# First head loaded and prepared in two parts, hash bits with a padded pitch, and two re-timed feed schedules in an attention + MoE kernel

## The chip, the cores and the metric

The kernel runs on one core of one Trainium2 chip. Engines are called as in the profile: PE is TensorE, PEld its weight loads, DVE is VectorE, ACT is ScalarE, POOL is GpSimd, SP issues most DMAs.

## The reference

Hash attention (4 batches, 8 heads, 768 tokens, head size 64) followed by a gated two-layer product on the attention output. Queries and keys are put in buckets by the signs of six projections; a query sees only the keys of its own bucket.

```python
q_bits = einsum('bhsd,dk->bhsk', q, proj) > 0          # same for k; 6 bits make a bucket
scores = where(q_bucket == k_bucket, q @ k.T / 8, -1e9)
attn   = exp(scores - max);  attn /= attn.sum() + 1e-9
x      = (attn @ v) -> [3072 tokens, 512]
h      = x @ w_in                                      # 512 -> 2048
out    = (h * sigmoid(h)) @ w_out                      # 2048 -> 512
```

## The kernel before

The work is a list of 288 units `w` (32 heads, nine units each). A unit is one score of 512 columns, one exponential on ACT, and four products with v ("AV") on PE. The sign bits of q and k are stacked under the values as extra rows, so one matmul gives value score and bucket test together. Everything else (transposes, bit projections, the MoE products of the batch before) is hung between the units: `plan(w, fn)` at fixed units, `moeq` as a queue of MoE pieces.

```python
def load_first(h):                       # first two heads: rows of q and k, on the SP queue
    for n, src in (("q", q), ("k", k)):
        nc.sync.dma_start(out=qk_sb[0, n][:, h], in_=src[0, h]...)
...
def proj_unit(*pairs):                   # bits of two pairs of heads, 768 columns
    bt = btp.tile([P, S], F16, tag="bits", name="bits")
    ...                                  # two PSUM tiles bp_ps (tag "m", 3 buffers), signs by DVE
def bits_unit(pairs, i, par):            # copy 13 x 768 bits under the values, on DVE
    nc.vector.tensor_copy(out=dst, in_=bits[pairs][r, :])
...
def mm1(ci, grp):                        # h = x @ w_in: 4 matmuls of 512 columns,
    hp = ps.tile([P, f, n], F32, tag="m", name="h_ps", bufs=3)   # same 3 PSUM buffers
    ...                                  # tanh on ACT, then g = (th + 1) * h on DVE
...
# the start: no unit can run before head 0's bits are there
t_first(0, 0, nc.scalar.copy); t_first(0, 1, nc.vector.tensor_copy)    # transposes of head 0
warm_up(2); bt = proj_first(0); v_unit(0, (0,))
...                                      # casts, bit copies of head 0
t_first(1, 0, nc.scalar.copy); t_first(1, 1, nc.vector.tensor_copy)    # transposes of head 1
warm_up(3)
...
for w in range(NW):                      # 3 scores lead
    for fn in at.pop(w, []): fn()
    ...
    skip = w % 3 == 2 or w % QST in (20, 21)    # QST = 36, BST = 72 units a batch
    if n == 1 and len(moeq) - keep < left and skip: n = 0
    for _ in range(n): moeq.popleft()()
    av(w); score(w + LEAD)
```

The softmax here doesn't subtract the row's maximum and nothing guards it: scores larger than these inputs give would overflow.

## Time and profile before

| | before |
|---|---|
| median | 306.18 us (305.82 to 306.61, 3 runs) |
| span of the profiled run | 304.06 us |
| bit copies on DVE (13 x 768) | 14 at 534 ns, 7 at 627 ns, 7 at 594 ns |

PE does something nearly all the time, so I measure everything by position: when the AV of a given unit starts. Four stretches follow: the start (up to the AV of unit 1, 10.29 us), units 1 to 54 (30.37 us), units 54 to 144 (71.77 us: the first quarter of MoE work has to be fitted in here), and the rest (191.63 us).

### The profile page before, as it was taken

To read this page: it belongs to the slowest core of one execution; us is meant where nothing else is said; L and a number is where in the kernel's file an instruction comes from. 1 tells how busy PE (TensorE), PEld (TensorE's weight loads), DVE (VectorE), ACT (ScalarE), POOL (GpSimd) and SP (SyncE) were. 2 spreads that over 40 slices of the span, in tenths; PEclk is the share of its full clock that TensorE was granted. 3 is DMA by queue.
4 is the path that set the end of the run, shared out by engine and by line. 5 is a ranking of instruction groups with operands and counts; after the bars stand their busy time and mean duration, and the time that the engine had idled before them with its cause. 6 is when DMAs were issued, how large, how long until landed. Compare 5 with 4: busy or idle time off the path is not lost.

```text
span 304.1 us, 7165 instructions
## 1 busy us (share of the span) xinstructions
PE 299.6 (99%) x2710; PEld 174.9 (58%) x2710; DVE 180.7 (59%) x341; ACT 210.7 (69%) x392; POOL 129.2 (42%) x203
## 2 busy tenths in 40 slices
PE   8999999999999999999999999999999999999996
PEld 3675855555666545555565665555566654446653
DVE  5697977799559344854696334853543442664332
ACT  5987989988877696978976766878877732442300
POOL 7589999377506851855148321765111100000000
PEclk9999999999999999999999999999999999999999
DMA  7999898999979838854068246011022013001112
GB/s 204 242 241 195 179 149 127 226 160 99 165 133 187 137 77 237 127 113 133 2 115 125 76 63 197 5 42 32 2 60 63 0 38 95 34 2 69 37 63 75
DMA packets 102786, 32.87 MB, mean 108 GB/s; under 512 B 90656, under 2 KB 99808, under 8 KB 102752
## 3 DMA queue, kind: packets, MB, share of 16 engines
q1 hardware_dynamic: 98368, 28.22, 44.6%
q0 software_dynamic: 4224, 4.19, 9.1%
q8 instruction: 21, 0.34, 0.5%
q14 instruction: 13, 0.11, 0.1%
q10 hardware_dynamic: 160, 0.00, 0.0%
HBM read 27.27 MB, written 6.29 MB: 110 GB/s over the span
## 4 chain that ended last, share of the span: by engine, by line
PE 95%; DVE 3%; ACT 1%; issue 0%; POOL 0%; ACTq 0%; POOLq 0%
PE h_ps L423 26%; PE o_ps L455 26%; PE s_ps L333 20%; PE o_ps L365 13%; PE bp_ps L279 3%; PE tp_ps L185 2%; PE o_ps L441 1%; PE warm_ps L125 1%; DVE g L429 1%; DVE qka L310 1%; ACT u L336 1%; PE bp_ps L225 1%; PE tp_ps L198 1%; PE o_ps L356 0%; DVE bits L285 0%
## 5 line engine op out<-in xcount | busy, mean ns | idle before, releaser
L336 ACT ACTIVATE u<-s_ps 128x512 f16<-128x512 f32 x288 | 156.4, 602 | 39.9 <-PE s_ps L333 39.4
L429 DVE SCALAR_TENSOR_TENSOR g<-th,h_ps 128x512 f16<-128x512 f32 x96 | 65.1, 683 | 75.4 <-ACT th L427 75.4
L423 PE MATMUL h_ps<-xT,win 128*128 128x512 f16 (+1 forms) x512 | 97.4, 325 | 0.1
L365 PEld LDWEIGHTS <-u 128*128 128x128 f16 x1152 | 67.6, 98 | 42.9 <-ACT u L336 11.2
L455 PE MATMUL o_ps<-wout,g 128*128 128x512 f16 x368 | 91.6, 379 | 0.0
L365 PE MATMUL o_ps<-vv,u 128*128 128x65 f16 x1152 | 82.8, 194 | 0.3
L427 ACT ACTIVATE th<-h_ps 128x512 f32<-128x512 f32 x96 | 57.3, 597 | 36.6 <-PE h_ps L423 33.5
L423 PEld LDWEIGHTS <-win 128*128 128x128 f16 x512 | 49.9, 98 | 31.8 <-issue 0.4
L385 POOL TENSOR_TENSOR x_pr<-osum,rec 128x384 f16<-128x384 f32 x23 | 19.0, 826 | 89.4 <-DVE rec L384 89.0
L455 PEld LDWEIGHTS <-g 128*128 128x128 f16 x368 | 35.8, 98 | 34.1
L333 PE MATMUL s_ps<-qka 71*128 71x512 f16 x192 | 52.7, 327 | 0.2 <-DVE qka L238 0.2
L333 PE MATMUL s_ps<-qkb 128*128 128x512 f16 x192 | 52.8, 326 | 0.0
L251 POOL TENSOR_SCALAR qka<-qk 64x1536 f16<-64x1536 f32 x15 | 22.0, 1465 | 12.1 <-DVE qk L246 6.8
L460 DVE TENSOR_SCALAR osb<-o_ps 128x512 f32<-128x512 f32 x23 | 15.8, 686 | 15.5 <-PE o_ps L455 15.5
L251 POOL TENSOR_SCALAR qkb<-qk 64x1536 f16<-64x1536 f32 x15 | 22.1, 1471 | 1.2
L262 POOL TENSOR_TENSOR vsa<-v_sb 128x192 f32<-128x192 f32 x32 | 19.3, 604 | 0.0
L260 POOL CAST vv<-v_sb 128x384 f16<-128x384 f32 x32 | 16.7, 520 | 0.9 <-DMA v_sb<-in_v_dram 0.5
L333 PEld LDWEIGHTS <-qka 71*128 71x128 f16 x192 | 15.4, 97 | 0.8 <-ACT qka L238 0.6
L246 DVE STREAM_TRANSPOSE qk<-k_blk 128x768 f32<-128x768 f32 x10 | 15.8, 1576 | 0.0
L246 DVE STREAM_TRANSPOSE qk<-q_blk 128x768 f32<-128x768 f32 x10 | 15.7, 1572 | 0.0
L333 PEld LDWEIGHTS <-qkb 128*128 128x128 f16 x192 | 15.4, 97 | 0.0
L379 DVE TENSOR_TENSOR osum<-o_ps,vsum 128x390 f32<-128x390 f32 x23 | 13.0, 565 | 2.3
(64 smaller groups left out, 164.8 us busy)
## 6 DMA issues: line engine op xcount, KB each, us to landing
out_dram<-osb SPq DMA_DIRECT2D x23, 256.0 KB
v_sb<-in_v_dram SPq DMA_DIRECT2D x15, 384.0 KB
q_blk<-in_q_dram SPq DMA_DIRECT2D x40, 96.0 KB
k_blk<-in_k_dram SPq DMA_DIRECT2D x40, 96.0 KB
win<-in_moe_w_in_dram POOLq DMA_DIRECT2D x4, 512.0 KB, 8.1
wout<-in_moe_w_out_dram POOLq DMA_DIRECT2D x4, 512.0 KB, 8.1
q_sb<-in_q_dram SPq DMA_DIRECT2D x5, 384.0 KB
k_sb<-in_k_dram SPq DMA_DIRECT2D x5, 384.0 KB
```

Source lines behind the costliest of these rows:

```text
L246: nc.vector.transpose(out=dst, in_=qk_sb[p, "qk"[n]])
L251: nc.gpsimd.tensor_scalar(out=dst[rows, :], in0=qk32[p][rows, :], scalar1=CS, scalar2=1.0, op0=ALU.mult, op1=ALU.mult)
L260: nc.gpsimd.tensor_copy(out=vv[:, :, 0:D], in_=src)
L262: nc.gpsimd.tensor_tensor(out=sa, in0=src[:, 0:3], in1=src[:, 3:6], op=ALU.add)
L333: nc.tensor.matmul(sp[:, o0 : o0 + n], t[rows, S + jt * P : S + (jt + 1) * P], t[rows, c0 : c0 + n], start=True, stop=True)
L336: nc.scalar.activation(out=u, in_=sp, func=AF.Exp, scale=ESC)
L365: nc.tensor.matmul(o_ps[h][:, c0 // P + i, :], u[:, o0 + i * P : o0 + (i + 1) * P], vv[:, jt, :], start=(not direct(h) and w % NU == 0 and ...
L385: (nc.vector if direct(h) else nc.gpsimd).tensor_tensor(out=x_pr[p][:, :, par * D : (par + 1) * D], in0=o[:, 0:NJ, 0:D], in1=rec[:, :, Non ...
L423: nc.tensor.matmul(hp[:, j, :], w_in16[:, dt, ft * P : (ft + 1) * P], xT[4 * b + dt][:, c0 : c0 + n], start=(dt == 0), stop=(dt == NDT - 1))
L427: nc.scalar.activation(out=th, in_=hp, func=AF.Tanh, scale=0.5)
L429: after.append(lambda: nc.vector.scalar_tensor_tensor(out=g[ci][:, grp * f : (grp + 1) * f, :], in0=th, scalar=1.0, in1=hp, op0=ALU.add, o ...
L455: nc.tensor.matmul(o2[tt], g[ci][:, ft, ct * P : (ct + 1) * P], w_out16[:, ft, :], start=(ft == 0), stop=(ft == NFT - 1))
```

## The change

Its intent: start the scores sooner by loading head 0 in two parts (two of three tile pairs first) with k on ACT's DMA queue beside q on SP's; keep DVE's bit copies to one port (the prediction says why), by giving the bits a pitch of 258; and fill two places where PE waits for ACT, by opening two MoE groups early (three of their four matmuls at units 66 and 70) and by spreading batch 1's MoE pieces evenly. The diff, cut:

```diff
 def load_first(h):
+    for c in ((slice(0, 4 * D), slice(4 * D, NJ * D)) if h == 0 else (slice(0, NJ * D),)):
         for n, src in (("q", q), ("k", k)):
-            nc.sync.dma_start(out=qk_sb[0, n][:, h], ...
+                (nc.scalar if (h, n) == (0, "k") else nc.sync).dma_start(
+                    out=qk_sb[0, n][:, h, c], ...
-    nc.scalar.dma_start(out=pw..., in_=proj)      # twice
+    nc.gpsimd.dma_start(out=pw..., in_=proj)      # twice, after the identity
...
-        bt = btp.tile([P, S], F16, tag="bits", name="bits")
+        bt = btp.tile([P, 3, CB + 2], F16, tag="bits", name="bits")      # CB = 256
-                nc.vector.tensor_copy(out=dst, in_=bits[pairs][r, :])
+                nc.vector.tensor_copy(out=dst, in_=bits[pairs][r, :, 0:CB])
...
-        def mm1(ci, grp):
+        def mm1(ci, grp, dts=slice(0, NDT)):      # may leave a group open after 3 of 4
...
-    t_first(0, 0, nc.scalar.copy)
-    t_first(0, 1, nc.vector.tensor_copy)
+    xa, xb = slice(0, 2), slice(2, 3)
+    t_first(0, 0, act, xa)                        # casts, k, then t_rest() for xb,
+    ...                                           # signs and bit copies by part
-    t_first(1, 0, nc.scalar.copy)                 # head 1 before the first scores
-    t_first(1, 1, nc.vector.tensor_copy)
+    plan(0, lambda: t_first(1, 0, act))           # head 1 behind them
+    plan(0, lambda: t_first(1, 1, vec))
-        plan(w0 + 20, lambda Q=Q: proj_unit(2 * Q, 2 * Q + 1))
+        wp = w0 + (24 if Q == 2 else 20)          # units 56 -> 60
+        plan(wp, lambda Q=Q: proj_unit(2 * Q, 2 * Q + 1))
+    for i in range(2):
+        plan(66 + 4 * i, first_units[0].pop(0))   # the two opened groups
...
         skip = w % 3 == 2 or w % QST in (20, 21)
+        if BST + 5 <= w < 2 * BST:
+            skip = w * 36 // 66 == (w - 1) * 36 // 66
```

I call its parts S (start), B (bits), H (opened groups), W (projection at unit 60) and P (even spacing); each can be applied alone.

## The prediction

> **What bounds the kernel now.** I read the page's busy table and chain of waits first, then a table of stretches, then the waits of two stretches, last the timeline of the first 10 us.
>
> ```profile
> PE 299.6 (99%) x2710; PEld 174.9 (58%) x2710; DVE 180.7 (59%) x341; ACT 210.7 (69%) x392; POOL 129.2 (42%) x203
> PE 95%; DVE 3%; ACT 1%; issue 0%; POOL 0%; ACTq 0%; POOLq 0%
> ```
>
> TensorE carries 95% of the chain. So the time is the first matmul (1.01 us), plus all TensorE work, plus every pause of TensorE, plus a tail of about 3 us. The change removes no TensorE work; it can only remove pauses and start earlier. Matmul busy (99%) hides the pauses because matmuls overlap, so I look where matmuls wait for weights, in the stretches where ScalarE (ACT) is full:
>
> ```profile
> 31.00:44.50 13.50, 13.50 (x180) 9.58 (x177) 11.69 (x19) 12.22 (x25) 12.66 (x16) 1.00 0.99 157
> 44.50:53.00 8.50, 8.48 (x105) 4.33 (x102) 6.33 (x15) 8.50 (x19) 7.87 (x18) 1.00 0.84 126
> ...
> 107.50:113.00 5.50, 5.39 (x62) 2.55 (x61) 2.13 (x7) 5.21 (x11) 3.54 (x8) 1.00 0.17 55
> ```
>
> The columns are us, then the busy time of PE, PEld, DVE, ACT, POOL. The first row is for contrast: ACT has 1.3 us to spare. From 44.5 to 53 ACT is busy 8.50 of 8.50 us and weight loads only 4.33; from 107.5 to 113 ACT has 5.21 of 5.50. The waits of these two stretches, in order:
>
> ```profile
> PEld L365 <- ACT u L336: 3.9, 15, 0.3
> ```
> ```profile
> PEld L365 <- ACT u L336: 2.6, 9, 0.4
> ```
>
> There the product with v (AV) waits for the exponential. One unit of attention is one exponential (ACT: 22 in 10.93 us, 0.50 each) but only a 512-column score and four AV matmuls on TensorE: in the timeline an AV group at 12.12 is followed by its score at 12.23 and the next work at 12.46, so 0.34. Between 44.05 and 53.15 lie 19 units: 9.10 - 19 x 0.34 - 0.67 (six transposes, two starting matmuls) = 2.0 us of pause. Between 107.87 and 112.43 lie 9: 4.56 - 9 x 0.34 = 1.5 us. A third such place, six units from 27.91 to 30.78, has 2.87 - 6 x 0.34 = 0.8 us. After 113 us I find none worth naming. Outside the start, then, some 5 us of pauses are all there is.
>
> The start:
>
> ```profile
> 1.01 2.31 PE L125 MATMUL warm_ps<-warm 128*128 128x512 bf16 x5 [1.01 <-POOL warm L114]
> ...
> 3.31 0.87 PE L198 MATMUL tp_ps<-ident,q_row 128*128 128x128 f32 x3
> ...
> 4.22 0.48 ACT L201 COPY qk<-tp_ps 128x384 f32<-128x384 f32 x1 [0.74 <-PE tp_ps L198]
> ...
> 6.44 0.68 DVE L228 TENSOR_SCALAR bits<-bp_ps,sc 128x384 f16<-128x384 f32 x1 [0.96 <-PE bp_ps L225]
> ...
> 7.15 0.70 DVE L238 COPY qka<-bits 7x384 f16<-7x384 f16 x2
> ...
> 8.00 0.81 PE L333 MATMUL s_ps<-qka 71*128 71x512 f16 x4 [0.16 <-DVE qka L238]
> ...
> 9.51 0.85 PE L225 MATMUL bp_ps<-qk,pw 128*32 128x384 f32 x8
> ...
> 10.29 0.30 PE L365 MATMUL o_ps<-vv,u 128*128 128x65 f16 x4
> ```
>
> A chain of dependent steps leads from the landing of q (transposes at 3.31) to the first score at 8.00. The second unit's AV starts at 10.29, behind head 1's bit projection (9.51).
>
> **What the Trainium skill says.** "TensorE: Matmul & The Clock Gate", section "What's actually happening": the array runs at half rate until about 3.4 us of activity. The trace agrees: five warm-ups of 512 columns start 0.43 us apart from 1.01, while 512-column matmuls later take 0.215 (four in 0.86 in the chain). "VectorE: DVE Perf Modes", section "What auto-detection actually checks": a 16-bit copy within SBUF takes four elements a cycle only if the outermost counts of source and destination are both even, or equal. "SBUF — State Buffer", section "Who interferes with whom": such a two-port copy excludes GpSimd for the whole instruction. The trace agrees: the 13x768 bit copies have minimum 351 ns, maximum 1591 ns, the long ones while GpSimd ran its 1465 ns casts. "DMA: Bandwidth & Descriptors", section "Issuing engines are not separate DMA queues": a second queue saves issue time only. Before, the SP issues of q and k start at 0.75 and 1.21, so 0.46 us is what it can save.
>
> **The change part by part.**
>
> Start, first head. Two of three tile pairs go first; k is issued by ACT beside q. The warm-ups (21 blocks of 128 columns at 0.107) keep TensorE until 1.01 + 2.25 = 3.25, so the q transposes start at about 3.25, no earlier than before. From there, sizes scaled from the rows above: second q transpose at 3.47, ACT copy 3.92 to 4.29 (256 columns, 0.37 instead of 0.48), k transposes to 4.12 and DVE copy 4.57 to 5.0; the last tile pair's transposes and a warm-up hold TensorE to 5.3; projection of 256 columns, bits ready at about 6.05 (before 6.44). Signs 0.53 instead of 0.68, two bit copies of 0.25 instead of 0.35: 7.2. First score at about 7.3, 0.7 earlier.
>
> But the second score needs q's last tile pair: signs of 128 columns (0.4) and two small copies (0.2 each) come behind on DVE, so 8.1 to 8.2. Exponentials then start at 7.7, 8.6 and 9.1. Head 1's transposes (6 x 0.109 = 0.65) were before done while TensorE waited for the bits; now they follow the third score, and the ACT copy of them (0.48) stands behind the third exponential in ACT's order: 9.6 to 10.1. On DVE the same copy stands behind a memset (0.70) and the identity's cast: also about 10.0. Head 1's projection cannot start before 10.1 (before 9.51), and AV of the second unit starts at 10.1 + 0.78 = 10.9 (before 10.29). So this part starts scores 0.7 us earlier and, by my reckoning, hands it back with about 0.6 more: +0.6. Up to 28 us TensorE has no pause that could absorb it. My queue times are uncertain by half a microsecond, with more room to be better than worse, so I put +0.4.
>
> Memsets of QKB and proj's load. The two GpSimd memsets (2.69 us in all) leave the start; GpSimd issues proj instead, ready before 5.3 by my estimate. Hidden: 0.
>
> Bits through one port. With pitch 258 the source is 3 rows of 256 and the destination one run, so 3 against 768: no two-port mode. 28 DVE copies: before 7.5 + 4.4 + 4.2 us with these waits in them = 16.1; after, estimated from the page's two elements a cycle, 768 / 2 / 0.96 = 400 ns plus the fixed 150 (351 - 200) = 550 ns each, 15.4 in sum. The outliers of 1.5 us go, but no pause of TensorE ended on them. Worth 0 to -0.1.
>
> Batch 0 spaced. Two three-quarter groups of the first product (3 x 0.216 = 0.65 us each) move to units 66 and 70, within the pause from 44.05 to 53.15. ACT is then about two exponentials behind (1.0 us), so 0.65 fits almost without starving it; the pause of 0.14 a unit refills it in four units. Gain 2 x 0.65 less some 0.15 = -1.15. Moving the projection of pairs 4 and 5 from unit 56 to 60 moves its ACT gap (1.08 us at 43.63) along: 0.
>
> Spacing in batch 1. 36 pieces over 66 units instead of two in three: before, they ran out at 107.5. Evenly spread, two units need 2 x 0.34 + 1.09 x 0.86 = 1.62 us of TensorE against 1.0 of ACT plus about 0.4 of tanh: no pause. Gain -1.4. Two waits of TensorE for DVE's g (0.25 us at 74.5, 0.23 at 101.6) are likely to shrink with the looser pace: -0.3.
>
> Sum: +0.4 - 1.15 - 1.4 - 0.3 = -2.45; 306.18 - 2.45 = 303.7 us.
>
> **The rivals.** First: the start is a real gain. For it: the first score does come earlier, and if head 1's copies find their engines free, the 0.7 stays: 302.6. Against it: the ACT order puts the copy behind three exponentials, and the second of these waits for bits that are made last. Second: the start costs more, because proj through GpSimd lands after 5.3 us or the clock rises later (projection at half rate, +0.4): 304.5. Third: a wait takes the place of the one removed. The two opened groups hold two of three PSUM buffers from unit 66 to 79, and the spread drops the rule that kept units 20 and 21 free for the projection, which wants two buffers. If transposes or projection then wait for DVE, half of the 2.85 returns: 305. For it: 0.23 us at 101.6 was such a wait. Against it: in units 66 to 79 only one transpose unit wants a buffer. Fourth: ACT is the true bound of batch 0 and fillers starve it; then the heads are worth nothing: 304.9. Against it: fillers are smaller than its backlog.
>
> **Range and chances.** All parts at their best (start -0.7, heads -1.3, spread -1.5, g waits -0.5) give 302.2; the start at +0.9, half of the rest lost, 305.2. Runs of before differ by 0.8 us. For 2% the change would have to take 6.1 us, more than all pauses I found outside the start; for slower by 2% it would have to add 6.1, for which nothing speaks. Predicted 303.7, range 302.2 to 305.2; faster 0.03, same 0.96, slower 0.01.
>
> **What would show it.** The first score near 7.3, the second near 8.2; head 1's projection after 10 us with the ACT copy just before it. ACT full from 44 to 53 with two groups of three h matmuls inside. No run of exponentials alone near 107 to 113. Bit copies all near 550 ns. Wrong if head 1's projection starts before 9.5, if TensorE waits for PSUM buffers in units 66 to 92, or if the pauses by ACT return elsewhere in batch 1.

## More of the kernel before

The metric is the device time of one execution in microseconds (us); medians are over several executions.

The prediction shows the lines of the profile before; one more is needed later, the stretch from 53 to 74 us (us, then busy time of PE, PEld, DVE, ACT, POOL):

```profile
53.00:74.00 21.00, 21.00 (x192) 11.28 (x191) 19.03 (x31) 19.03 (x38) 14.46 (x19) 1.00 1.14 173
```

The reader is to see DVE at 19.03 of 21.00 us.

## The result, and the profile after

| | before | after |
|---|---|---|
| median, same rounds | 306.0 us (305.73 to 306.61, 4 runs) | 306.74 us (306.53 to 307.02, 4 runs) |
| span of the profiled run | 304.06 | 304.90 |
| first score / AV of unit 1 | 8.00 / 10.29 | 8.21 / 11.85 |
| units 1 to 54 | 30.37 | 30.36 |
| units 54 to 144 | 71.77 | 71.05 |
| unit 144 to the end | 191.63 | 191.64 |

The ratio is 1.0022, 95% interval 1.0004 to 1.0040: a little slower, well inside 2%. All ratios here are the mean time of one kernel's fast runs over that of the kernel before's fast runs of the same rounds, so not quite the ratio of the medians quoted. The whole difference of the spans, 0.84 us, lies in two stretches: +1.56 in the start and -0.72 between units 54 and 144. The prediction had +0.4 and -2.85 there.

The page's busy line and the chain, after:

```profile
PE 298.3 (98%) x2719; PEld 176.3 (58%) x2719; DVE 181.4 (59%) x346; ACT 210.0 (69%) x394; POOL 129.8 (43%) x208
PE 90%; DVE 6%; ACT 2%; issue 1%; POOL 0%; DVEq 0%; ACTq 0%; POOLq 0%
```

DVE's share of the chain has doubled from 3% to 6%. That is the first hint: the pauses did not vanish, they changed owner. The two stretches in which PE waited for ACT (the first is taken 1.5 us later, as the start is longer), and the waits for the exponential from 44 to 56 us:

```profile
46.00:54.50 8.50, 8.37 (x108) 4.79 (x101) 7.35 (x15) 7.03 (x15) 7.80 (x19) 1.00 0.80 123
...
107.50:113.00 5.50, 5.50 (x64) 3.87 (x62) 1.86 (x5) 4.77 (x10) 4.10 (x9) 1.00 0.09 25
```
```profile
PEld L393 <- ACT u L364: 2.1, 7, 0.4
ACT u L364 <- PE s_ps L361: 1.5, 3, 1.1
```

At 107.5 weight loads rose from 2.55 to 3.87 us and PE is busy throughout: the run of bare exponentials is gone, as predicted. At 46 to 54.5 ACT is no longer full (7.03 of 8.50): it waits 1.1 us during the projection, which now lies in this stretch, and twice more for a score, behind the opened groups. PE's waits for the exponential fell from 3.9 to 2.1 us only. New waits, between 56 and 82 us (total, times, longest):

```profile
PEld L393 <- ACT u L364: 0.9, 2, 0.7
PE h_ps L456 <- DVE g L465: 0.8, 2, 0.6
PEld bp_ps L305 <- DVE g L465: 0.6, 2, 0.4
```

The last two are waits for a PSUM buffer that DVE's `g` frees. On PE's timeline the larger one is the last bracket here:

```profile
66.70 1.50 PE L305 MATMUL bp_ps<-qk,pw 128*32 128x512 f32 x16
68.80 1.02 PE L456 MATMUL h_ps<-xT,win 128*128 128x512 f16 x4 [0.60 <-DVE g L465]
```

The start, after, on PE and on DVE (start us, us, what, and in brackets the idle time before it and what ended it):

```profile
3.48 0.66 PE L203 MATMUL tp_ps<-ident,q_row 128*128 128x128 f32 x2
...
5.70 1.51 PE L245 MATMUL bp_ps<-qk,pw 128*32 128x256 f32 x16
...
8.21 0.39 PE L361 MATMUL s_ps<-qka 71*128 71x512 f16 x1 [0.55 <-DVE qka L262]
9.13 0.59 PE L361 MATMUL s_ps<-qka 71*128 71x256 f16 x3 [0.54 <-DVE qka L262]
9.57 0.49 PE L203 MATMUL tp_ps<-ident,q_row 128*128 128x128 f32 x3
...
11.06 0.85 PE L245 MATMUL bp_ps<-qk,pw 128*32 128x384 f32 x8 [0.17 <-ACT qk L207]
11.85 0.30 PE L393 MATMUL o_ps<-vv,u 128*128 128x65 f16 x4
```
```profile
6.84 0.54 DVE L253 TENSOR_SCALAR bits<-bp_ps,sc 128x256 f16<-128x256 f32 x1 [0.77 <-PE bp_ps L245]
7.42 0.74 DVE L262 COPY qka<-bits 7x256 f16<-7x256 f16 x2
8.19 0.41 DVE L253 TENSOR_SCALAR bits<-bp_ps,sc 128x128 f16<-128x128 f32 x1
8.63 0.45 DVE L262 COPY qka<-bits 7x128 f16<-7x128 f16 x2
```

The signs start at 6.84 us, later than before (6.44) instead of at the predicted 6.05, so the first score gained nothing; and from the first score to the AV of unit 1 it takes 3.64 us instead of 2.29, because of the second bit chain (8.19 to 9.08 on DVE) and of head 1's transposes at 9.57, whose ACT copy has to pass two exponentials before head 1's projection can run at 11.06.

### The profile page after: what moved, and what is told of

Read it like the earlier page. It is cut to its first block, busy times and chain, and to the rows that moved or that the text cites. A ratio compares the mean times of both kernels' runs of the same rounds, so it can differ in the third digit from the quotient of the medians.

```text
span 304.9 us, 7211 instructions
## 1 busy us (share of the span) xinstructions
PE 298.3 (98%) x2719; PEld 176.3 (58%) x2719; DVE 181.4 (59%) x346; ACT 210.0 (69%) x394; POOL 129.8 (43%) x208
## 4 chain that ended last, share of the span: by engine, by line
PE 90%; DVE 6%; ACT 2%; issue 1%; POOL 0%; DVEq 0%; ACTq 0%; POOLq 0%
PE o_ps L491 26%; PE h_ps L456 24%; PE s_ps L361 18%; PE o_ps L393 11%; PE bp_ps L305 3%; DVE g L465 2%; PE tp_ps L190 2%; ACT u L364 1%; PE o_ps L477 1%; PE warm_ps L128 1%; DVE qk L270 1%; DVE qka L338 1%; PE bp_ps L245 1%; PE o_ps L384 0%; DVE qkb L335 0%
## 5 line engine op out<-in xcount | busy, mean ns | idle before, releaser
L463 ACT ACTIVATE th<-h_ps 128x512 f32<-128x512 f32 x96 | 58.0, 604 | 38.0 <-PE h_ps L456 35.4
L456 PEld LDWEIGHTS <-win 128*128 128x128 f16 x512 | 49.8, 98 | 32.2 <-issue 1.5
L361 PEld LDWEIGHTS <-qka 71*128 71x128 f16 x192 | 15.4, 97 | 1.8 <-DVE qka L262 0.9
L361 PEld LDWEIGHTS <-qkb 128*128 128x128 f16 x192 | 15.4, 97 | 0.0
```

The source lines that it names most:

```text
L361: nc.tensor.matmul(sp[:, o0 : o0 + n], t[rows, S + jt * P : S + (jt + 1) * P], t[rows, c0 : c0 + n], start=True, stop=True)
L456: nc.tensor.matmul(hp[:, j, :], w_in16[:, dt, ft * P : (ft + 1) * P], xT[4 * b + dt][:, c0 : c0 + n], start=(dt == 0), stop=(dt == NDT - 1))
L463: nc.scalar.activation(out=th, in_=hp, func=AF.Tanh, scale=0.5)
```

## The experiments

Seventeen kernels ran, all correct. Stretches are given as start (AV of unit 1) and units 54 to 144; the other two are constant (30.36 and 191.6) unless said. A median is followed by that of the kernel before in the same rounds. Stretches come from one profiled execution each. From unit 1 on, equal schedules agree within about 0.1 us; the start doesn't: the start of the kernel before, unchanged, took from 10.15 to 11.12 us in the eight profiles that have it.

### Everything but the start

The changed kernel with the start of before: parts B, H, W and P.

```diff
-    (the changed start: loads, warm-ups, proj by GpSimd, two parts, head 1 behind)
+    (the start of the kernel before, lines unchanged)
```

> The changed kernel with the start of the kernel before (one load of the first head, k by the sync queue, proj by ACT, memsets and head 1's transposes before the first scores); bits, opened groups, projection at unit 60 and the spacing of batch 1 as changed. Theory A (the losses add up along TensorE): the second unit's AV was 1.56 us later in the changed kernel (11.85 against 10.29) and stayed 1.55 later up to unit 54, so this run is 1.5 us faster than the changed kernel: about 305.2, some 0.8 us under the kernel before. Rival (an ACT-bound stretch between 42 and 57 us swallows what the start gives): about 306.5, nothing gained.

Measured: 305.4 (before 305.96), ratio 0.9977 [0.9964, 0.9990]. Start 10.15, units 54 to 144 71.03. Against the changed kernel's ratio of 1.0022 the start costs 0.0045 x 306 = 1.4 us, and the other four parts together save 0.7 us where I had summed up 2.85. This is what theory A expected (305.2).

### The start alone

Part S on the kernel before.

```diff
+    (the changed start only; bits, opened groups, projection and spacing as before)
```

> The kernel before with the new start alone. Theory A: 1.5 us slower than the kernel before, about 307.6, with the first score near 8.2 and the second unit's AV near 11.8. If the late clock (full rate only from about 6.8 us in the changed kernel, 5.3 before) was chance and not caused by the new start, the first score is near 7.7 and the loss near 1.0. Rival (prediction as worked out): loss 0.4 to 0.6.

Measured: 308.06 (305.96), ratio 1.0079 [1.0056, 1.0102]. Stretch 54 to 144 71.75, as before. So 2.4 us are lost, more than any expectation had. The profiled run, at 310.41, was the slowest of the six, with proj landing so late that the first projection waited for it until 6.38 us, and with the clock at half rate until 13.61 us by the trace's clock records. Its start of 14.07 is not a typical one. Outside the start it lost 0.59 us between units 1 and 54 (30.95), which comes back below in the run with the old bit copies.

### Without the opened groups

The changed kernel without H.

```diff
-            first = [lambda grp=grp: mm1(0, grp, head) for grp in range(2)] + ...
-        plan(66 + 4 * i, first_units[0].pop(0))
+    (groups opened and closed at once, as before)
```

> The changed kernel without the two opened groups at units 66 and 70. Theory B (their gain is given back: ACT gaps of 0.18 and 0.19 behind them and a 0.57 us wait of TensorE at 57.2, where the tanh of the closed groups comes into a stretch that ACT already fills): same as the changed kernel within 0.4 us, 306.4 to 307.1. Rival (prediction): 1.15 us slower, 307.9.

Measured: 307.33 (305.96), ratio 1.0049 [1.0027, 1.0070], a little outside both expectations. That is 0.0027 x 306 = 0.8 us slower than the changed kernel, with overlapping intervals; the six times scatter from 306.77 to 308.90, and the profiled one was among the fast. The profile shows only 0.10 us in the stretch (71.15 against 71.05), so here the groups help by 0.10, made of a gain and a new wait that has nothing to do with MoE:

```profile
53.70 0.51 PE L425 MATMUL xt_ps<-ident,x_pr 128*128 128x128 f16 x6 [0.50 <-DVE x_pr L413]
```

Six transposes of the attention output wait for DVE. So "without H" is not the clean inverse of "with H"; the effect of H has to be read beside another base (below).

### Keeping units 20 and 21 free

The changed kernel, with the old rule for the projection's units kept beside the spacing.

```diff
-            skip = w * 36 // 66 == (w - 1) * 36 // 66
+            skip = w * 36 // 66 == (w - 1) * 36 // 66 or w % QST in (20, 21)
```

> The changed kernel with the rule put back in batch 1 that no piece of the MoE runs in units 20 and 21 of a group of four heads, beside the even spacing. Theory C (the 0.76 us wait at 68 us is a matmul of h for a PSUM buffer that DVE frees late behind the projection): that wait goes and the run is about 0.7 us faster, 306.0. Rival (DVE is the bound there and the wait moves to the next piece): within 0.2 us of the changed kernel.

Measured: 306.6 (305.96), ratio 1.0016 [1.0004, 1.0028]; stretch 71.03 against 71.05. The wait of 0.60 us ahead of the matmul at 68.80 is gone, and one of 0.80 us for the same `g` of DVE stands ahead of a matmul at 74.29 instead. (The 0.76 of the expectation is the same 0.60, counted from an earlier end of the matmul before it than the profile models.) The rival held. Rival three of the prediction named the wait correctly, but the dropped rule is not its cause: the buffer comes back late wherever the piece is put.

### Head 1 first again

The changed kernel, with only head 1's transposes moved back ahead of the first scores.

```diff
+    t_first(1, 0, act)
+    t_first(1, 1, vec)
     nc.vector.memset(QKB[1][0:64, :], 0.0)
...
-    plan(0, lambda: t_first(1, 0, act))
-    plan(0, lambda: t_first(1, 1, vec))
```

> The changed kernel with head 1's transposes and their two copies (and no other part of the start) put back ahead of the first scores. Theory A1 (of the 1.55 us, 1.35 arise between the first score and the second unit's AV, because head 1's copy on ACT stands behind three exponentials: 3.64 us there against 2.29 before): the stretch from the first score to the second AV shrinks from 3.6 to about 2.6 and the run to about 305.6, 1.1 us under the changed kernel. Rival A2 (the loss lies ahead of the first score, in the late landing of proj and of the bits): the run stays within 0.4 us of the changed kernel.

Measured: 306.01 (305.94), ratio 1.0005 [0.9988, 1.0021]; start 10.79 instead of 11.85, although here PE had to wait 0.63 us for proj at 6.00. From first score to AV of unit 1: 2.74 us instead of 3.64. By the profile this is the larger half of the start's loss; in timed runs it is 0.0017 x 306 = 0.5 us, with overlapping intervals, where theory A1 had 1.1.

### The changed kernel with the old bit copies

Parts S, H, W and P, not B.

```diff
-        bt = btp.tile([P, 3, CB + 2], F16, tag="bits", name="bits")
+        bt = btp.tile([P, S], F16, tag="bits", name="bits")
```

> The changed kernel with the bits back in rows without a gap, so that DVE copies them through two ports. Theory D (the copies at 0.54 us each lengthen DVE's queue behind the projection, on which the waits of 0.76 and 0.37 us at 68 and 76 us rest): these waits shrink by about 0.4 in sum, 306.3. Rival (prediction: no wait of TensorE rests on the copies; copies blocked by GpSimd take as long): within 0.15 us of the changed kernel.

Measured: 306.99 (305.94), ratio 1.0044 [1.0021, 1.0068]: no faster, though the stretch 54 to 144 is 0.55 shorter (70.50). The profiled run lost that elsewhere. Units 1 to 54 took 30.97, because a transpose, due at about 39 us, waited for a copy by DVE; and PE's clock fell back to half rate after it had been up:

```profile
PE tp_ps L190 <- DVE qk L192: 0.4, 1, 0.4
```
```profile
6.44 0.86 PE L245 MATMUL bp_ps<-qk,pw 128*32 128x256 f32 x16 [0.43 <-DVE qka L232]
...
10.09 0.85 PE L203 MATMUL tp_ps<-ident,q_row 128*128 128x128 f32 x3
```

The projection ran at full rate (0.86, where the changed kernel's profile has 1.51), but the three transposes after the pauses ahead of the two scores did not: in the changed kernel they take 0.49. From the second score to the AV of unit 1 it took 4.08 us instead of 2.72, so the start of this run, 13.49, holds some 1.4 us of lost clock. The trace's clock records say the same: full rate from 6.18 us, half rate from 9.59, full rate again from 13.01.

The wait at 39 us matters for B. Both profiles of the new start with old bit copies have it (30.95 and 30.97 from unit 1 to 54), and none of the other seventeen does (30.36 to 30.47). On DVE's timeline two bit copies of 1.57 and 1.53 us, each beside a cast of GpSimd, stand ahead of the late copy. With the old start such copies lie a little earlier in DVE's order and nothing waits. So beside the new start the padded bits cost 0.55 us between units 54 and 144 and save 0.61 before unit 54: in sum nothing, and the timed runs show no gain from taking them out. The same 0.6 is part of why the new start alone loses 2.4 us and only 1.4 beside the other parts. One rival stays: these two runs were also the two latest to start (14.07 and 13.49), so the lateness and not the copies may have moved things. What B costs beside the old start needs another base (below).

### The spacing alone

Part P on the kernel before.

```diff
+        if BST + 5 <= w < 2 * BST:
+            skip = w * 36 // 66 == (w - 1) * 36 // 66
```

> The kernel before with the even spacing of batch 1 alone. Theory C (1.5 us of waits for the exponential at 107 to 113 us go; about 0.7 us come as a wait for a PSUM buffer behind the projection, because the rule for units 20 and 21 fell): 0.6 us faster than the kernel before, 305.4. Prediction as worked out: 1.7 us faster, 304.3. Rival (what spacing gives is all handed back to DVE): 306.0.

Measured: 304.65 (305.94), ratio 0.9953 [0.9939, 0.9967], so 1.4 us saved; stretch 70.12 against 71.77, so 1.65 by the profile. Two lines of code do nearly all the good that the change does. Theory C missed: its new wait of 0.7 us for a PSUM buffer did not come, and the prediction's 304.3 was near. Of the two waits for `g` that the prediction let shrink, the one near 74.5 us went (0.15 us by unit 78) and the one behind the projection stayed (0.98 us on PEld, before and after).

### The spacing with units 20 and 21 kept free

```diff
+            skip = w * 36 // 66 == (w - 1) * 36 // 66 or w % QST in (20, 21)
```

> The kernel before with the even spacing and with units 20 and 21 still kept free. If the wait behind the projection is the only one handed back: 1.3 us faster than the kernel before, 304.7. If it only moves (in the changed kernel with the rule it came back as 0.96 us at 73 us), no better than the spacing alone: 305.4.

Measured: 304.77 (305.94), ratio 0.9962 [0.9946, 0.9978]; stretch 70.46, with waits of 0.20 and 0.22 us for `g` ahead of the matmuls at 72.67 and 74.60. Without the rule there is no such wait: the even spacing does not need it.

### proj by ACT's queue

The changed kernel, with proj issued by ACT (behind k) instead of GpSimd.

```diff
+    nc.scalar.dma_start(out=pw[0:64, 0:NBIT], in_=proj)
+    nc.scalar.dma_start(out=pw[64:128, NBIT + 1 : 2 * NBIT + 1], in_=proj)
...
-    nc.gpsimd.dma_start(out=pw[0:64, 0:NBIT], in_=proj)
-    nc.gpsimd.dma_start(out=pw[64:128, NBIT + 1 : 2 * NBIT + 1], in_=proj)
```

> The changed kernel with proj loaded by ACT's queue (behind the two parts of k) and not by GpSimd's. Theory E (in four of five profiles with the new start the first bit projection began at 6.0 to 6.4 us and waited for proj, which landed 3.4 to 4.1 us after its issue): the projection begins at 5.7 or earlier and the run is 0.4 us faster than the changed kernel, 306.3, with fewer slow runs. Rival (the clock of TensorE and the order of the bits set the start): within 0.15 us of the changed kernel.

Measured: 306.98 (306.18), ratio 1.0030 [1.0015, 1.0045]. In the profile the wait for proj is gone, the projection starts at 5.85 behind an ACT copy instead, and the start is 11.34, 0.51 shorter; the timed runs show no gain at all. The profile says where it went: 0.11 us more between units 1 and 54 (30.47), 0.07 between 54 and 144 (71.12) and 0.35 after unit 144 (191.99). The last lies behind the last matmul, in the semaphore waits with which SP closes the program, and all three runs with proj by ACT beside the split load have it (191.99 to 192.01). So this run clears proj's route only of the total, not of the start.

### The start with three things mended

The changed kernel with head 1 first, proj by ACT, and the last tile pair copied in two pieces.

```diff
+    t_first(1, 0, act); t_first(1, 1, vec)            # before the scores
-        nc.scalar.copy(out=qk32[0][:, 0 : 2 * HS]...[:, :, 2 * P : 3 * P], in_=tp)
+        for n in range(2):
+            nc.scalar.copy(out=qk32[0][:, n * HS + 2 * P : n * HS + 3 * P], in_=tp[:, n])
```

> The changed kernel with three mendings of its start: head 1's transposes ahead of the first scores, proj by ACT's queue, and the last tile pair of q and k copied by two copies that do not span the columns of the first two, so that the projection need not wait for them. If the causes add up: first score near 7.5, second AV near 10.2, the run 0.4 us under the one with head 1 first alone (306.01), 305.6. Rival (the split of the first head is no gain in itself: the second score waits for bits made last): first score earlier, second AV no earlier than 10.7, 306.0.

Measured: 306.15 (306.18), ratio 1.0000 [0.9985, 1.0015]; start 10.90. No better than head 1 first alone, as the rival had it (0.35 us of it is the close of the program again, 191.99). The q transposes still began only at 3.62 us, waiting for q to land, proj, now behind k, ended another wait at 6.12, and first scores came at 8.15. That pointed to the loads.

### The spacing with padded bits

Parts P and B on the kernel before.

```diff
+        if BST + 5 <= w < 2 * BST: ...
-        bt = btp.tile([P, S], F16, tag="bits", name="bits")
+        bt = btp.tile([P, 3, CB + 2], F16, tag="bits", name="bits")
```

> The kernel before with the even spacing and the bits through one port. Theory D2 (28 copies at 0.54 us lengthen DVE's queue after each projection; from unit 54 to 144 the changed kernel took 71.05 us and with two-port bits 70.50): 0.5 us slower than the spacing alone, 305.2, by longer waits of TensorE for DVE between 66 and 78 us. Rival (prediction: worth 0 to -0.1): 304.6.

Measured: 305.43 (306.18), ratio 0.9968 [0.9949, 0.9987]; stretch 70.58 against 70.12 for P alone. B costs 0.46 us by the profile, 0.0015 x 306 = 0.5 by the ratios (whose intervals overlap). I had it at 0 to -0.1. Up to unit 96 the AV of single units comes level with P alone; by unit 105 it is 0.45 later. There, ahead of a matmul at 75.39 us, stands a wait that P alone doesn't have:

```profile
PE h_ps L427 <- DVE g L433: 0.2, 1, 0.2
```

### The spacing with the projection at unit 60

Parts P and W on the kernel before.

```diff
+        wp = w0 + (24 if Q == 2 else 20)
+        if BST + 5 <= w < 2 * BST: ...
```

> The kernel before with the even spacing and the projection of pairs 4 and 5 at unit 60 in place of 56. Theory F (the bits of these pairs are then in DVE's queue when the last tile of x is due at unit 74, and TensorE waits for it; 0.66 us of such a wait in the run without opened groups): 0.5 us slower than the spacing alone, 305.2. Rival (prediction: the gap moves along, 0): 304.6.

Measured: 304.33 (306.18), ratio 0.9945 [0.9929, 0.9961]; stretch 70.11. W is worth nothing beside P, as predicted, but this is the best version found: 0.5% faster than the kernel before, and faster than the changed kernel. It also lets the bit copies be compared in a profile. The eight copies of pairs 6 and 7 on DVE, here in the old form:

```profile
67.76 1.25 DVE L310 COPY qka<-bits 13x768 f16<-13x768 f16 x2
...
69.64 0.50 DVE L310 COPY qkb<-bits 13x768 f16<-13x768 f16 x1
70.16 0.41 DVE L307 TENSOR_SCALAR qkb<-bits,sc 13x768 f16<-13x768 f16 x1
70.58 1.07 DVE L310 COPY qka<-bits 13x768 f16<-13x768 f16 x2
...
72.41 0.39 DVE L310 COPY qkb<-bits 13x768 f16<-13x768 f16 x1
72.81 0.42 DVE L307 TENSOR_SCALAR qkb<-bits,sc 13x768 f16<-13x768 f16 x1
```

and in the changed kernel, in the padded form:

```profile
69.95 1.10 DVE L338 COPY qka<-bits 13x768 f16<-13x768 f16 x2
...
71.69 0.53 DVE L338 COPY qkb<-bits 13x768 f16<-13x768 f16 x1
72.23 0.60 DVE L335 TENSOR_SCALAR qkb<-bits,sc 13x768 f16<-13x768 f16 x1
72.85 1.10 DVE L338 COPY qka<-bits 13x768 f16<-13x768 f16 x2
...
74.70 0.54 DVE L338 COPY qkb<-bits 13x768 f16<-13x768 f16 x1
75.26 0.61 DVE L335 TENSOR_SCALAR qkb<-bits,sc 13x768 f16<-13x768 f16 x1
```

The sums are 4.04 and 4.48 us, a difference of 0.44, close to the loss of 0.46 beside P alone. From 56.09 to 77.30 us DVE has no idle bracket in the first kernel at all (from 58.26 to 79.94 in the changed one). In this stretch DVE is full and PE waits for its results, so what its copies grow by comes back as waits.

### k of the first head beside q, and nothing else

The kernel before with one line changed.

```diff
-            nc.sync.dma_start(out=qk_sb[0, n][:, h],
+            (nc.scalar if (h, n) == (0, "k") else nc.sync).dma_start(out=qk_sb[0, n][:, h],
```

> The kernel before with one difference: k of the first head goes by ACT's queue, ahead of proj, beside q. Theory G (the two queues share the same DMA engines, so q lands with k and not ahead of it): q's transposes begin at 3.55 to 3.75 us instead of 3.31 to 3.44, k's no earlier than 3.9, and the run is the same as the kernel before or slower (306.0 to 306.5). Rival (prediction: the second queue saves k's issue time): k's transposes 0.2 or more earlier and the run up to 0.4 faster.

Measured: 307.49 (306.01), ratio 1.0052 [1.0040, 1.0065]: 1.6 us lost to a change of queue, more than theory G had. The profile:

```profile
4.42 0.87 PE L198 MATMUL tp_ps<-ident,q_row 128*128 128x128 f32 x3 [1.09 <-DMA q_row<-in_q_dram]
...
9.85 0.81 PE L333 MATMUL s_ps<-qka 71*128 71x512 f16 x4
```

The q transposes start at 4.42 instead of 3.31 because q lands at least 1.1 us later, and the first score at 9.85 instead of 8.00. The other 0.7 us goes with the clock, which rose at 8.55 us here and at 5.14 in the kernel before. The DMA records show the two loads side by side: k's 192 KB move from 1.76 to 3.68 us on ACT's queue, the first 192 KB of SP's queue from 2.08 to 3.44, against 1.78 to 3.05 in the kernel before. One thing is not separated: without k, SP also issues the loads behind q earlier (v at 1.21 instead of 1.68 us, q of head 1 at 1.68 instead of 2.31), and these share the engines too.

### The mended start with k back on SP's queue

```diff
-                (nc.scalar if (h, n) == (0, "k") else nc.sync).dma_start(
+                nc.sync.dma_start(
```

> The run with the mended start (head 1 first, proj by ACT, two last copies; 306.15) with k's two parts back on the sync queue behind q's. Theory G: q's first part lands near 3.1 and its transposes begin as soon as the warm-ups end (3.25), first score near 7.8, the run about 0.2 faster, 305.9. Rival (the split itself sets the loss: two sign steps and twice the small copies on DVE put the second score 0.9 us behind the first whatever lands when): first score earlier or not, second AV no earlier than 10.6, 306.1.

Measured: 306.02 (306.01), ratio 1.0001 [0.9988, 1.0014]; start 10.44.

```profile
3.22 0.64 PE L203 MATMUL tp_ps<-ident,q_row 128*128 128x128 f32 x2
...
7.79 0.52 PE L203 MATMUL tp_ps<-ident,k_row 128*128 128x128 f32 x3 [0.89 <-DMA k_row<-in_k_dram]
8.14 0.81 PE L361 MATMUL s_ps<-qka 71*128 71x512 f16 x4
```
```profile
5.99 0.54 DVE L253 TENSOR_SCALAR bits<-bp_ps,sc 128x256 f16<-128x256 f32 x1 [0.41 <-PE bp_ps L245]
6.57 0.49 DVE L262 COPY qka<-bits 7x256 f16<-7x256 f16 x2
```

Now the first part runs as I had worked it out: transposes at 3.22 (3.25), signs at 5.99 (6.05), bit copies of 0.25 each, done at 7.06. But four SP issues for head 0 come ahead of head 1's loads, k of head 1 lands at 7.8, and its transposes, which stand ahead of the scores in PE's order, keep the first score to 8.14. The gain of the split was there and went to a later transfer. Two more things hide in the equal times: 0.37 us of this run are the close of the program (192.01), and the fair base is not the kernel before but the changed kernel with the old start (0.9977), against which the mended start still loses 0.7 us in timed runs.

### The spacing with opened groups

Parts P, W and H on the kernel before, bits in the old form.

```diff
+    (opened groups at units 66 and 70, on top of the spacing and the projection at 60)
```

> The kernel before with the even spacing, the projection at unit 60 and the opened groups; old start, two-port bits. Theory H (DVE is full from 57 to 77 us, so what TensorE does early is waited for there, and the early tanh add 0.57 us): from unit 54 to 144 70.5 us, as against 70.1 without the opened groups, and the run 0.4 us slower than that one (304.33): 304.7. Rival (prediction: the opened groups give 1.15): 303.2.

Measured: 304.64 (306.01), ratio 0.9959 [0.9947, 0.9971]; stretch 70.52 against 70.11 for P and W, as theory H had it. H costs 0.41 us by the profile, 0.0014 x 306 = 0.4 by the ratios, whose intervals overlap. Its way can be followed by the AV of single units, in us after that of unit 54:

| unit | P, W | P, W, H | difference | what happens |
|---|---|---|---|---|
| 65 | 6.60 | 6.60 | 0 | |
| 66 | 7.09 | 7.59 | +0.50 | first group of three matmuls (0.65) |
| 69 | 8.56 | 8.84 | +0.28 | some regained from ACT's pause |
| 70 | 9.05 | 9.84 | +0.79 | second group |
| 76 | 11.99 | 12.56 | +0.57 | |
| 79 | 14.75 | 14.10 | -0.65 | both groups need one matmul instead of four |
| 80 | 15.09 | 15.01 | -0.08 | wait for an exponential |
| 92 | 26.96 | 27.37 | +0.41 | wait for `g` |

```profile
PEld L365 <- ACT u L336: 1.1, 3, 0.7
...
PE h_ps L428 <- DVE g L437: 0.6, 1, 0.6
```

The groups did gain 0.65 us for two units. Then the tanh of the early groups delayed an exponential, and whatever PE was early for, DVE was not ready.

### Two bit copies moved from DVE to ACT

On P and W.

```diff
+            elif p in (6, 7) and par == 0 and n == 0:
+                nc.scalar.copy(out=dst, in_=bits[pairs][r, :])
```

> The kernel before with the even spacing, the projection at unit 60, and two of the eight bit copies of pairs 6 and 7 given to ACT in place of DVE. Theory H: DVE's full stretch is 0.8 us shorter; the waits of TensorE in it were only 0.28 there, so from unit 54 to 144 at most 0.3 us less than 70.1, the run 304.1. Rival (ACT has no room there and TensorE waits for the exponential instead): 304.5 or more.

Measured: 305.44 (306.01), ratio 0.9987 [0.9975, 0.9999], 1.3 us worse than without; stretch 71.32. The wait for `g` did not become a gain; PE waits for ACT instead:

```profile
70.21 0.30 PE L367 MATMUL o_ps<-vv,u 128*128 128x65 f16 x4 [0.20 <-ACT u L338]
72.66 0.30 PE L367 MATMUL o_ps<-vv,u 128*128 128x65 f16 x4 [0.73 <-ACT u L338]
```

ACT has no room there either. Around 70 us both ACT and DVE are close to full, and moving these copies only moved the wait.

### The changed kernel with k back on SP's queue

One line, everything else as changed.

```diff
-                (nc.scalar if (h, n) == (0, "k") else nc.sync).dma_start(
+                nc.sync.dma_start(
```

> The changed kernel with one line changed: k's two parts go back to the sync queue, each behind q's part of the same tiles. Theory (k beside q on a second queue delays q's landing, and this is the step of the prediction that failed at the start): q's first transposes start at 3.2 to 3.3 us instead of 3.5 or later, the second score follows the first by about 0.2 instead of 0.9, the first score is at 7.5 to 8.1, AV of the second unit at 10.9 to 11.4 (changed kernel 11.85), and the run is 0.4 to 0.8 us shorter than the changed kernel: 305.9 to 306.3 beside a kernel before of 306.0. Rival (the rest of the start, head 1's copies behind the exponentials, sets AV of the second unit, whatever the queues): AV of the second unit stays within 0.2 of 11.85 and the run within 0.2 of 306.7.

Measured: 306.35 (306.18), ratio 1.0007 [0.9985, 1.0029], so 0.0015 x 306 = 0.5 us better than the changed kernel, with overlapping intervals. Of the expectation, the transposes and the first score (8.05) hold; the second score and the AV of unit 1 do not, and the run lies just above its range:

```profile
3.22 0.64 PE L203 MATMUL tp_ps<-ident,q_row 128*128 128x128 f32 x2
...
5.65 1.49 PE L245 MATMUL bp_ps<-qk,pw 128*32 128x256 f32 x16
...
8.98 0.59 PE L361 MATMUL s_ps<-qka 71*128 71x256 f16 x3 [0.54 <-DVE qka L262]
```

The q transposes start at 3.22. But the second score still comes 0.93 after the first: that gap belongs to the two-part bit chain and not to the queue, and in the mended start it was merely hidden, as the first score was itself held back. And in this profiled run the sixteen projection matmuls took 1.49 us (0.86 in the run with head 1 first), so the clock was late (7.00 us by the clock records, though 7.23 in the changed kernel's own profile), and of the 0.26 us won by the load 0.16 reached the AV of unit 1 (11.69, against 11.85). There the rival held, which had that AV within 0.2 of 11.85. The share of the queue is between 0.16 (this profile) and 0.5 us (the timed runs). The load of proj, issued at the same times (1.49 and 2.26 us), landed 2.5 us after its issue here and 3.4 in the changed kernel.

## Why the prediction was wrong

I predicted 303.7 us (302.2 to 305.2) and measured 306.74. The spacing was right; the start and the opened groups were not, and the bits were right only where two effects cancel.

| part | predicted | profile | read from |
|---|---|---|---|
| start | +0.4 | +1.56 | changed against before |
| spacing, with `g` waits | -1.7 | -1.65 | spacing alone against before |
| projection at unit 60 | 0 | 0 | best version against spacing alone |
| bits through one port | 0 to -0.1 | +0.46 | spacing with padded bits against spacing alone (beside the new start: +0.55 - 0.61) |
| opened groups | -1.15 | +0.41 | beside spacing and unit 60, against the same without (in the changed kernel: -0.10) |

The rows add up to 0.78; the spans differ by 0.84. The sizes come from single profiles, so they carry the scatter of the clock at the start (below); the parts between units 54 and 144 do not, and the timed ratios agree with them within their intervals. The parts do not add freely: padded bits with the projection at unit 60 but without opened groups gave 71.15, as a wait for the attention output came in, and the bits' sign depends on the start. That the rows come near the whole is partly luck.

**Start: the step that failed is "the last tile pair's transposes and a warm-up hold TensorE to 5.3; projection of 256 columns, bits ready at about 6.05", with the loads taken as free ahead of it.** Signs came at 6.84, and the two bit copies behind them took 0.37 us each instead of 0.25. The other half, the hand-back, was right in mechanism and size: I had the first score at 7.3 and the AV of unit 1 at 10.9, 3.6 us apart, and the trace has 3.64. Moving head 1 back ahead of the scores shortened that to 2.74. So the missing microsecond lies before the first score. Three things in it are shown. First, the second queue: beside k, q landed later in every run (transposes at 3.48 to 3.75 us in the changed start, 3.22 with one queue), and with whole heads, as in the kernel before, this change alone cost 1.1 us at the landing and 1.6 us in time. Second, the projection waited for proj, which I had ready before 5.3, until 6.00 to 6.38 us in four of the profiles (rival two had it), or for ACT's copy of the last tile pair until 5.65 to 5.85. Third, the clock: the first projection took 1.51 us instead of 0.86 in the changed kernel's profile. Rival two had that as well. The +1.56 is not all schedule: full clock came at 7.23 us in this profile and at 5.14 in that of before, and the unchanged start took 11.08 in the profile whose clock also came at 7.23 (spacing with padded bits), 0.77 less than 11.85. With the clock early (4.98 and 4.73) the changed start still took 11.80 and 12.02. What remains is not settled: with head 1, proj and the queue mended, signs are on time at 5.99, but head 1's k then lands later. How the loss in timed runs (1.4 us beside all other parts, 2.4 alone) divides between load and clock from run to run I cannot say: the queue's part was measured as 0.16 to 0.5 us in the changed kernel.

**Opened groups: the step that failed is "0.65 fits almost without starving it; the pause of 0.14 a unit refills it in four units".** Of 1.30 us put in, 0.57 still stood at unit 76, where I had allowed 0.15. And I had taken the gain at the far end as kept: from 56 to 77 us it meets a DVE that has no idle time, so PE ended up waiting for `g` and for one exponential. Rival three was the right one, though not by its own reason (the dropped rule): with the rule kept, the wait only moved. Rival four, ACT as the true bound, covers part of it, as the experiment of moving two copies to ACT shows, but DVE was the bound I had not named.

**Bits: the step that failed is the term "15.4 in sum" against 16.1.** It is nearly right as a total (15.6 by the groups of the changed kernel), but a total is the wrong quantity. In the kernel before, the 1.5 us copies that it removes (at 18.6, 30.6 and 32.2 us) lie where nothing waited; the eight copies that it lengthens, from 4.04 to 4.48 us, lie in the one stretch where DVE is full. Beside the new start, where PE did wait in the stretch with the long copies, the sum came out within my 0 to -0.1, by luck.

**Spacing and projection: right**, the first in place (no run of exponentials alone near 107 us) and nearly in size, though one of the two waits for `g` stayed, the second in size.

**The range.** Its upper end took a start of +0.9 and half of the rest lost. It had no case in which both fillings, of the pause in batch 0 and of DVE, were worth less than nothing.

## What to carry to other kernels

Before filling a pause of one engine with work, look in the same stretch at every engine that the new work feeds: where another is nearly full (here DVE, 19.03 of 21.00 us), the time gained can come back as a wait for it, and 0.44 us over eight copies counted there, while the total over the kernel said nothing. A second DMA queue is not a second set of wires: put what the chain needs first alone at the head, and count what each early transfer pushes back behind it. And apply parts of a change one at a time, on more than one base; here two lines of schedule held nearly the whole gain (0.5%) and the rest cost more than that.

## What the Trainium skill lacked or had wrong

- "DMA: Bandwidth & Descriptors", section "Issuing engines are not separate DMA queues": I read it as "a second queue saves a little issue time and does no harm". It says that the DMAs interleave, and the runs show what that costs: with k of the first head issued beside q, q landed at least 1.1 us later (transposes at 4.42 instead of 3.31) and the run took 307.49 instead of 306.01 us. The same page's section "Queues, rings and completion order" says that each DMA engine takes turns between the queue rows it has work for; that fits the trace, in which the two queues' first 192 KB move at the same time (1.76 to 3.68 and 2.08 to 3.44 us), but no warning for a load that a chain waits for is drawn from it.
- "TensorE: Matmul & The Clock Gate", section "What you observe": the rise of the clock "around 4µs into sustained matmul activity, ±500ns run-to-run". Here, with matmuls from 1.0 us on, it scattered more: by the clock records that seventeen of the nineteen traces hold, full rate came between 3.89 and 8.55 us, and at 13.61 in one. With the same warm-up it was there for the sixteen projection matmuls at 6.0 us in one run (0.86 us), absent at 5.65 in another (1.49), and in a third there at 6.44 (0.86) but gone again for the transposes at 10.09 (0.85 instead of 0.49). The page's next section, "What's actually happening", does call the count of slow matmuls run-variable, which fits better. Why it came when it did, no run here shows.
- No page weighs the price of leaving the shared port against the waits that it saves, though the time of a copy in each mode can be estimated from the pages (the prediction's 0.55 was right: the one-port copies took 0.53 to 0.61 us each). Here the old copies took 0.35 to 0.42 us where GpSimd left them alone and up to 1.59 where it did not; one port made the first some 0.2 us longer and ended the second, which was worth +0.46 us beside the old start and about nothing beside the new one.
